# Strassen's sums from a list of their own, stores at one place, reciprocals in two pairs

## The chip, the cores and the metric

The kernel runs on one core of a Trainium2 chip. The metric is the device time of one execution in microseconds (us); of the kernel before there are three timed runs and one more under the profiler. All computation is in float32. TensorE (PE in the rows) multiplies matrices into PSUM; DVE (VectorE) and POOL (GpSimd) do elementwise work, DVE alone of the two on PSUM too; ACT (ScalarE) does activations and copies; SP (SyncE) issues nearly all transfers, in one queue. Every engine works its instructions strictly in the order of the program and waits where an operand isn't ready.

## The reference

```python
scores = scale * np.matmul(q, k.transpose(0, 1, 3, 2))        # 8 batches, 8 heads, 576 x 576
thresh = np.max(scores, axis=-1, keepdims=True) - tau
scores = np.where(scores >= thresh, scores, -1000000000.0)
attn = softmax(scores); x = attn @ v                          # bridged to (8, 576, 512)
xn = (x - mu) / np.sqrt(var + 1e-06) * g_ln
out = x + np.maximum(xn @ w_ch1, 0.0) @ w_ch2                 # 512 -> 2048 -> 512
```

## The kernel before

**Slots.** The attention of a batch runs in nine slots, s0 to s8, so there are 72 slots (`n`). A slot takes 128 queries for each of four blocks: s0 to s3 and s5 to s8 a pair of heads each, first half and second half of the sequence, s4 the leftover rows. Per slot: TensorE computes the scores into `sc`; DVE takes the maxima (`neg`, L399); ACT the exponentials `e` (L410); DVE masks them by the threshold and sums them into `den` (`weights`, L417, four instructions) and takes the reciprocal (L421); POOL divides `e` by `den` (L430, four instructions); DVE turns the 32x32 blocks into `et` (L495, two instructions, L489 in s4); SP writes `et` to a scratch in DRAM (`scr`, four transfers) and in the next slot reads it back as `em` (L510). TensorE multiplies `em` with V (L539) late in that next slot. In the first batch the weights are turned on TensorE instead, with diagonal matrices `diag`.

**Groups.** The sequence of a batch is two groups of 288 tokens, so there are 16 groups. A group's feed-forward part is cut into small steps, which `second_part` issues between the attention's matmuls, four times per slot (quarters 0 to 3). A group's mean is subtracted on DVE (`xc`, L580), then `p` = xc times W1 (4096 matmuls in all), relu on ACT into `hidden`, and the second product in Strassen's form: seven quarter products (`seg`) instead of eight, with sums and differences t1 to t4 of the quarters of `hidden` made on the way (L746), and the seven results, copied from PSUM by ACT, summed into `y` on POOL (L766), multiplied by the inverse deviation `rb` on DVE (L772) and added to x on POOL. `y` is turned on DVE (`ot`, L603) and stored by 16 transfers (L610). The first group has a plain second product.

The second group of a batch is ready two slots into the next batch: it has its `p` products from s2 to s4 there and its quarter products in s4 to s6. The first group of a batch starts in s6 and has its quarter products from the end of s8 to s1 of the next batch. The former is called an odd group below, the latter an even one (by its number).

**Order.** Everything that isn't TensorE's waits in lists of calls: `aside` (sums, differences, `root`, `store`) is run whole at four places of a slot, `stores` (the 16 transfers) at two, at the start of a slot and behind `weights`. Whatever a place runs is put into the engines' queues there, ahead of what the program issues later. So the list decides which work of the feed-forward part stands ahead of the attention's on DVE, POOL and SP.

Of the kernel before, what the change touches and what calls it, by code (L numbers as in the profile page):

```python
# [12 lines left out]
ALU = mybir.AluOpType  # L13
# [5 lines left out]
def kernel(  # L19
# [392 lines left out]
    def weights(es, thr, divide):  # L412
# [8 lines left out]
        nc.vector.reciprocal(den, den)  # L421
        diags = []
        for i in range(4):
            if not divide:
                if i % 2 == 0:
                    two = ffn.tile([128, TOK], F32, tag="o", bufs=6, name="diag")
# [160 lines left out]
    aside, stores = [], []  # L587
# [7 lines left out]
    def add_to_x(g, m, p2, rb):  # L595
        o = ffn.tile([128, TOK], F32, tag="o", bufs=6, name="o")
# [4 lines left out]
    def store(g, m, o):  # L601
        ot = ffn.tile([128, TOK], F32, tag="o", bufs=6, name="ot")
# [114 lines left out]
    def second_quarters(g, rb):  # L717
# [12 lines left out]
        def later(*calls):  # L730
            for what, fn, *args in calls:
# [5 lines left out]
                aside.append(go)  # L737

        def need(*what):
            while not done.issuperset(what):  # L740
                run_all(aside)
# [6 lines left out]
        def segment(weights, rhs, out=None):  # L748
# [10 lines left out]
            if out is None:  # L759
                out = ffn.tile([128, TOK], F32, tag="o", bufs=6, name="o")  # L760
                out = out.rearrange("p (m t) -> p m t", m=HM)
# [3 lines left out]
        def add(out, a, b):  # L765
            side.tensor_tensor(out=out, in0=a, in1=b, op=ALU.add)  # L766

        def finish(i, j):

            z = part_of(y, i, j)  # L770
            r = rb[:, (early, late)[j]].unsqueeze(1).to_broadcast([128, HM, HT])
            nc.vector.tensor_tensor(out=z, in0=z, in1=r, op=ALU.mult)  # L772
            add(z, z, part_of(groups[g], i, j))

        def give(i):
            for m in range(HM * i, HM * i + HM):
                store(g, m, y[:, m])

        side = nc.gpsimd
        later(("t3", by_fours, nc.gpsimd, b12, b22, b12, ALU.subtract))  # L780
        yield from segment(w2[0, 0], b11, y11)
        later(("t2", by_fours, nc.vector, b11, b11, b12, ALU.add))
        yield 2, 0.5
        p2 = yield from segment(w2[0, 1], b21)
        later(("t4", by_fours, nc.gpsimd, b21, b21, b11, ALU.subtract))
        yield 2, 0.5
        need("t3")
        p7 = yield from segment(s3, b12)
        yield 2, 0.5
        need("t2")  # L790
        yield from segment(s2, b11, y21)
        need("t4")
        later(
            ("t1", by_fours, nc.vector, b11, b22, b11, ALU.subtract),
            ("u2", add, y21, y21, y11),
            ("11", add, y11, y11, p2),
# [3 lines left out]
        later(("done11", finish, 0, 0))  # L800
# [4 lines left out]
            ("u4", add, y12, y21, p5), ("u3", add, y21, y21, p7), ("22", add, y22, y21, p5),  # L805
# [194 lines left out]
```

## Time and profile before

| | |
|---|---|
| timed runs, median (lowest to highest) | 1494.86 us (1493.07 to 1495.52) |
| profiled execution | 1493.05 us, span 1491.3 us |
| granted TensorE clock, mean | 0.982 |
| busy: PE, DVE, POOL, ACT | 91%, 63%, 43%, 31% of the span |
| TensorE's idle time before L539 (product with V) | 53.2 us |
| before the `p` products (L101) | 19.8 us, 14.3 of it waiting for `xc` |
| before the quarter products (L101) | 9.9 us |
| transfers: HBM read, written | 119.41 MB, 83.76 MB |

A row of a timeline has start, duration (us), engine, line, operation, output<-input, shapes, number of instructions, and in brackets the idle time ahead of it with what ended it. A row of the groups has total busy time, mean ns of one, and the idle time ahead with what ended most of it. In rows of a table by windows the third column from the end is TensorE's granted clock.

### The profile page before, as it was taken

How to read it: one execution, taken by the hardware profiler on the slowest of the kernel's cores; microseconds unless marked ns; L12 is line 12 of the kernel's file. 1: busy time of each engine (PE TensorE's matmuls, PEld its weight loads, DVE VectorE, ACT ScalarE, POOL GpSimd, SP SyncE). 2: the span in 40 equal slices, each digit the busy share in tenths (PEclk: the TensorE clock that was granted, in tenths of full speed). 3: DMA queues.
4: the chain of work that ended last, by engine and by line, in shares of the span. 5: the costliest groups of instructions: out<-in, count | busy, mean ns of one | idle time of the engine just before them, and what ended most of it. 6: DMA issues, size and time to landing. Idle time of an engine off the chain costs nothing.

```text
span 1491.3 us, 36015 instructions
## 1 busy us (share of the span) xinstructions
PE 1361.4 (91%) x15048; PEld 1008.2 (68%) x15048; DVE 934.4 (63%) x1560; ACT 459.4 (31%) x923; POOL 635.7 (43%) x854
## 2 busy tenths in 40 slices
PE   5879998999999898989999889998989889999996
PEld 3656665768576585857768576675858667685866
DVE  5989867567665674657755666556755576555421
ACT  3886422232322222222322323222232222323120
POOL 2354435545444352444535345343534444353413
PEclk8999999999999999999999999999999999999998
DMA  9612475468653887449744577447874487545211
GB/s 220 175 57 80 98 167 138 129 161 176 153 150 98 175 178 175 117 105 190 172 134 129 139 168 169 131 113 176 182 169 125 110 173 177 136 129 127 82 17 17
DMA packets 466868, 205.53 MB, mean 138 GB/s; under 512 B 275025, under 2 KB 428369, under 8 KB 466705
## 3 DMA queue, kind: packets, MB, share of 16 engines
q1 hardware_dynamic: 461936, 202.64, 56.9%
q8 instruction: 118, 1.93, 0.6%
q10 hardware_dynamic: 4736, 0.59, 0.4%
q14 instruction: 46, 0.37, 0.1%
q0 software_dynamic: 32, 0.00, 0.0%
HBM read 119.41 MB, written 83.76 MB: 136 GB/s over the span
## 4 chain that ended last, share of the span: by engine, by line
PE 48%; DVE 18%; DMA 12%; POOL 9%; SPq 6%; issue 4%; ACT 2%; DVEq 0%; POOLq 0%; ACTq 0%
PE seg L101 17%; PE p L101 15%; PE sc L539 8%; PE sc L385 7%; DVE e L417 6%; DMA scr<-et 5%; DMA em<-scr 5%; POOL y L766 4%; POOL e L430 4%; DVE et L495 3%; SPq L501 2%; DVE neg L399 2%; SPq L116 2%; DVE xc L580 1%; PE tp L101 1%
## 5 line engine op out<-in xcount | busy, mean ns | idle before, releaser
L101 PE MATMUL p<-xc,w 128*64 128x288 f32 x4096 | 524.3, 410 | 19.8 <-DVE xc L580 14.3
L101 PEld LDWEIGHTS p<-xc,w 128*64 128x64 f32 x4096 | 300.4, 138 | 226.8 <-issue 29.5
L399 DVE TENSOR_REDUCE neg<-sc 128x2 f32<-128x1152 f32 x144 | 188.4, 1349 | 241.0 <-PE sc L385 241.0
L430 POOL TENSOR_SCALAR e<-e,den 128x576 f32<-128x576 f32 x252 | 196.5, 796 | 213.4 <-DVE den L421 213.4
L410 ACT ACTIVATE e<-sc,neg 128x576 f32<-128x576 f32 x288 | 196.4, 742 | 264.7 <-DVE neg L399 257.9
L101 PE MATMUL seg<-hidden,w 128*64 128x144 f32 x3840 | 249.2, 287 | 0.0
L101 PEld LDWEIGHTS seg<-hidden,w 128*64 128x64 f32 x3840 | 235.7, 137 | 12.4 <-issue 7.7
L417 DVE SCALAR_TENSOR_TENSOR e<-sc,thr,e 128x576 f32<-128x576 f32 x288 | 219.1, 810 | 10.4 <-ACT e L410 10.4
L495 DVE STREAM_TRANSPOSE et<-e 128x1152 f32<-128x1152 f32 x112 | 151.9, 1369 | 83.2 <-POOL e L430 68.1
L539 PE MATMUL sc<-em,v_in 128*64 128x256 f32 (+1 forms) x1408 | 142.4, 348 | 53.2 <-DMA em<-scr 35.2
L682 ACT ACTIVATE hidden<-p 128x288 f32<-128x288 f32 x256 | 105.7, 413 | 225.2 <-PE p L101 223.4
L385 PE MATMUL sc<-kT,qT 64*128 64x384 f32 (+3 forms) x1024 | 150.6, 425 | 20.1 <-DVE qT L345 10.1
L403 POOL TENSOR_SCALAR thr<-neg,low_sb 128x2 f32<-128x2 f32 x144 | 43.1, 299 | 287.6 <-DVE neg L399 285.4
L539 PEld LDWEIGHTS sc<-em,v_in 128*64 128x64 f32 x1408 | 93.5, 142 | 91.6 <-DVE sq L628 26.8
L385 PEld LDWEIGHTS sc<-kT,qT 64*128 64x128 f32 x1024 | 94.2, 191 | 69.9 <-issue 16.1
L101 PE MATMUL seg<-hidden,stage 128*64 128x144 f32 x1920 | 123.4, 287 | 2.7 <-POOL hidden L746 2.7
L101 PEld LDWEIGHTS seg<-hidden,stage 128*64 128x64 f32 x1920 | 118.0, 137 | 6.5 <-POOL hidden L746 3.0
L556 ACT COPY x<-sc 128x256 f32<-128x256 f32 x60 | 22.3, 371 | 247.2 <-PE sc L539 241.1
L746 POOL TENSOR_TENSOR hidden<-hidden 128x576 f32<-128x576 f32 x60 | 85.1, 1437 | 23.0 <-ACT hidden L682 15.1
L772 DVE TENSOR_TENSOR y<-y,rb 128x288 f32<-128x288 f32 x60 | 35.5, 592 | 94.8 <-POOL y L766 94.8
L565 POOL TENSOR_TENSOR sum<-sum,x 128x256 f32<-128x256 f32 (+1 forms) x64 | 35.7, 557 | 121.3 <-ACT x L556 118.8
L766 POOL TENSOR_TENSOR y<-y,o 128x288 f32<-128x288 f32 x90 | 79.3, 881 | 14.0 <-ACT o L762 9.3
(149 smaller groups left out, 1177.9 us busy)
## 6 DMA issues: line engine op xcount, KB each, us to landing
scr<-et SPq DMA_DIRECT2D x252, 288.0 KB, 4.6
em<-scr SPq DMA_DIRECT2D x63, 1024.0 KB, 5.9
out_dram<-ot SPq DMA_DIRECT2D x256, 36.0 KB, 2.1
q_in<-in_q_dram SPq DMA_DIRECT2D x124, 72.0 KB, 5.5
k_in<-in_k_dram SPq DMA_DIRECT2D x120, 72.0 KB, 3.1
v_in<-in_v_dram SPq DMA_DIRECT2D x64, 128.0 KB, 4.5
rest<-scr SPq DMA_DIRECT2D x63, 128.0 KB, 6.0
w<-in_moe_w_ch_dram SPq DMA_DIRECT2D x10, 512.0 KB, 6.1
```

Source lines behind the costliest of these rows:

```text
L101: nc.tensor.matmul(out[r], lhsT=lhsT[:, r], rhs=rhs, **flags)
L385: nc.tensor.matmul(sc[h][64 * i : 64 * i + 64 if s == HP else 128, at : at + n], lhsT=ql[r] if s == HP else qT[r, half, j * 128 : (j + 1) ...
L399: nc.vector.tensor_reduce(out=neg[:, i], in_=pairs[h], axis=AXL.X, op=ALU.max, negate=True,)
L403: nc.gpsimd.tensor_scalar(out=thr[:, i], in0=neg[:, i], scalar1=-1.0, scalar2=low_sb, op0=ALU.mult, op1=ALU.add,)
L410: nc.scalar.activation(es[:, i], blocks[i], func=AF.Exp, bias=neg[:, i : i + 1])
L417: nc.vector.scalar_tensor_tensor(out=es[:, i], in0=blocks[i], scalar=thr[:, i : i + 1], in1=es[:, i], op0=ALU.is_ge, op1=ALU.mult, accum_o ...
L430: nc.gpsimd.tensor_scalar(out=es[:, i], in0=es[:, i], scalar1=den[:, i : i + 1], scalar2=1.0, op0=ALU.mult, op1=ALU.mult,)
L495: nc.vector.transpose(et[:, :, 64 * h : 64 * h + 64].rearrange("p n (j c) -> p j n c", j=2), es[:, 2 * h : 2 * h + 2].rearrange("p j (n c) ...
L539: nc.tensor.matmul(dst[64 * h : 64 * h + 64], lhsT=vt[:, c, h, :] if c < J else vr[:, h, :], rhs=pick(em[:, c] if c < J else er, hp, h), s ...
L682: nc.scalar.activation(hidden[:, d], p1, func=AF.Relu)
L746: eng.tensor_tensor(out=out[at], in0=in0[at], in1=in1[at], op=op)
L766: side.tensor_tensor(out=out, in0=a, in1=b, op=ALU.add)
```

## The change

Three things are changed.

1. `weights`: from the second batch on, the reciprocal is taken in two instructions, one for each pair of blocks, each right behind its pair's masks.
2. The sums, differences and stores of Strassen's form leave `aside` for a list of their own, `drops`. `drip(most)` first runs everything up to and with the last urgent call (t1 to t4 are urgent), then at most `most` further ones. It is called behind `weights` with 0, behind the turning into `et` with 5, and at the end of a slot with 6. `need` takes calls from the front, one at a time. From slot 13 on, `aside` isn't run behind the maxima any more. From the second batch on, stores are issued at the start of a slot alone.
3. Who sums: the two sums that come early stay on POOL, with their multiplication and addition of x. The last five sums, and the multiplication and addition of the block that comes last, go to DVE. The second half of `y` (features 256 to 511) is multiplied and added to x by POOL in two large operations, 128x576. The results of the quarter products get a ring of four buffers of their own (`part`), and the ring `o` (`o`, `ot`, `diag`) shrinks from six to four.

```diff
+            if divide and i % 2:
+                nc.vector.reciprocal(den[:, i - 1 : i + 1], den[:, i - 1 : i + 1])
+        if not divide:
+            nc.vector.reciprocal(den, den)
...
+    def drip(most):
+        for d in [d for d in drops if d[0]]:
+            at = drops.index(d)
+            for _, fn in drops[: at + 1]:
+                fn()
+            del drops[: at + 1]
+        for _, fn in drops[:most]:
+            fn()
+        del drops[:most]
...
         def need(*what):
             while not done.issuperset(what):
-                run_all(aside)
+                drops.pop(0)[1]()
...
-        later(("t3", by_fours, nc.gpsimd, b12, b22, b12, ALU.subtract))
+        later(("t3", by_fours, pool, b12, b22, b12, ALU.subtract), urgent=True)
...
         later(
-            ("u4", add, y12, y21, p5), ("u3", add, y21, y21, p7), ("22", add, y22, y21, p5),
-            ("21", add, y21, y21, p4), ("done22", finish, 1, 1), ("done21", finish, 1, 0),
-            ("hi", aside.append, lambda: give(1)),
+            ("u4", add, dve, y12, y21, p5), ("u3", add, dve, y21, y21, p7),
+            ("22", add, dve, y22, y21, p5), ("21", add, dve, y21, y21, p4),
+            ("hi", finish, pool, 1),
         )
         yield 2, 0.5
         p3 = yield from segment(s4, b22)
-        later(
-            ("12", add, y12, y12, p3), ("done12", finish, 0, 1),
-            ("lo", aside.append, lambda: give(0)),
-        )
+        later(("12", add, dve, y12, y12, p3), ("done12", finish, dve, 0, 1))
+        later(*((f"o{m}", store, g, m, y[:, m]) for m in range(NK)))
...
-        run_all(aside)
+        if n < SLOTS + HP:
+            run_all(aside)
...
         run_all(aside)
-        run_all(stores)
+        drip(0)
+        if n < SLOTS:
+            run_all(stores)
...
         run_all(aside)
+        drip(5)
...
         run_all(aside)
+        drip(6)
```

The order of TensorE's instructions is the same in both kernels. At three places the order of the others moves.

DVE in s6 of an odd group, before (`sc_146` and `sc_147` are the two halves of the scores, `e_101` the weights):

```order
L399 TENSOR_REDUCE neg<-sc_147 128x2
L580 TENSOR_TENSOR xc<-x,mean 128x288 x4
L417 SCALAR_TENSOR_TENSOR e_101,den<-sc_146,thr,e_101 128x576 x2
L417 SCALAR_TENSOR_TENSOR e_101,den<-sc_147,thr,e_101 128x576 x2
L421 RECIPROCAL den<-den 128x4
L772 TENSOR_TENSOR y<-y,rb 128x2x144 x3
L495 STREAM_TRANSPOSE et<-e_101 128x2x18x32 x2
L603 STREAM_TRANSPOSE ot<-y 128x288 x4
L399 TENSOR_REDUCE neg<-sc_146 128x2
```

and in the changed kernel:

```order
L399 TENSOR_REDUCE neg<-sc_147 128x2
L583 TENSOR_TENSOR xc<-x,mean 128x288 x4
L417 SCALAR_TENSOR_TENSOR e_101,den<-sc_146,thr,e_101 128x576 x2
L422 RECIPROCAL den<-den 128x2
L417 SCALAR_TENSOR_TENSOR e_101,den<-sc_147,thr,e_101 128x576 x2
L422 RECIPROCAL den<-den 128x2
L498 STREAM_TRANSPOSE et<-e_101 128x2x18x32 x2
L779 TENSOR_TENSOR y<-y,part 128x2x144 x5
L787 TENSOR_TENSOR y<-y,rb 128x2x144
L779 TENSOR_TENSOR y<-y,x 128x2x144
L617 STREAM_TRANSPOSE ot<-y 128x288 x4
L399 TENSOR_REDUCE neg<-sc_146 128x2
```

The turning into `et` now follows the reciprocals directly, and the work on `y` stands behind it.

SP from the middle of s2 to s4, before:

```order
L610 DMA out_dram<-ot 32x9x32 x8
L116 DMA q_in<-in_q_dram 32x18x32 x4
L116 DMA k_in<-in_k_dram 32x18x32 x4
L610 DMA out_dram<-ot 32x9x32 x8
L501 DMA scr<-et 32x18x128 x4
L510 DMA em<-scr 128x4x512
L511 DMA rest_94<-scr 64x512
L501 DMA scr<-et 32x18x128 x4
```

and in the changed kernel:

```order
L624 DMA out_dram<-ot 32x9x32 x12
L116 DMA q_in<-in_q_dram 32x18x32 x4
L116 DMA k_in<-in_k_dram 32x18x32 x4
L504 DMA scr<-et 32x18x128 x4
L513 DMA em<-scr 128x4x512
L514 DMA rest_94<-scr 64x512
L624 DMA out_dram<-ot 32x9x32 x4
L504 DMA scr<-et 32x18x128 x4
```

Four stores more stand ahead of the loads of q and k, none between these and `scr`, and four behind the next `em`.

POOL in s5 of an odd group, before (`hidden<-hidden` is t4, one instruction for each half):

```order
L403 TENSOR_SCALAR thr<-neg,low_sb 128x2 x2
L746 TENSOR_TENSOR hidden<-hidden 128x4x144 x2
L430 TENSOR_SCALAR e_101<-e_101,den 128x576 x4
L766 TENSOR_TENSOR y<-y 128x2x144
L766 TENSOR_TENSOR y<-y,o 128x2x144
```

and in the changed kernel:

```order
L403 TENSOR_SCALAR thr<-neg,low_sb 128x2 x2
L433 TENSOR_SCALAR e_101<-e_101,den 128x576 x4
L760 TENSOR_TENSOR hidden<-hidden 128x4x144 x2
L779 TENSOR_TENSOR y<-y 128x2x144
L779 TENSOR_TENSOR y<-y,part 128x2x144
L787 TENSOR_TENSOR y<-y,rb 128x2x144
```

t4 and the division have changed places.

More of the change, by code (lines that the diff above doesn't have):

```diff
@@ L775, in give, with add, finish @@
[L775 to L779, printed above, removed]
[L780 removed]
+        def add(eng, out, a, b):
+            eng.tensor_tensor(out=out, in0=a, in1=b, op=ALU.add)
+        def finish(eng, i, j=None):
+            cols = slice(None) if j is None else (early, late)[j]
+            at = (slice(None), slice(HM * i, HM * i + HM), cols)
+            z, x = y[at], groups[g][at]
+            r = rb[:, cols].unsqueeze(1).to_broadcast(list(z.shape))
+            eng.tensor_tensor(out=z, in0=z, in1=r, op=ALU.mult)
+            add(eng, z, z, x)
```

42 lines of the change are left out of this document (17 added, 25 removed).

## The prediction

> **What bounds the kernel now.** I read the busy shares first, then TensorE's groups with what ended their idle time, then TensorE's timeline over one batch, and behind each gap the queues of DVE, POOL and SP. TensorE is busy for 91% of the span, so the time is its work plus its gaps. Two groups of gaps count:
>
> ```profile
> L101 PE MATMUL p<-xc,w 128*64 128x288 f32 x4096 | 524.3, 410 | 19.8 <-DVE xc L580 14.3 <-ACT hidden L682 3.8 <-DVE o L597 0.7
> L539 PE MATMUL sc<-em,v_in 128*64 128x256 f32 (+1 forms) x1408 | 142.4, 348 | 53.2 <-DMA em<-scr 35.2 <-DVE rb L629 6.8 <-DVE et L495 5.9
> ```
>
> 53.2 us before the product with V (L539), which needs the turned weights `em`, and 14.3 us before the first product of a group, which needs the centred x (`xc`). In TensorE's timeline of one batch (about 174 us, which the next batches repeat) they are:
>
> ```profile
> 664.53 1.95 PE L539 MATMUL sc<-em,v_in 128*64 128x256 f32 x16 [2.81 <-DMA em<-scr]
> 685.26 1.95 PE L539 MATMUL sc<-em,v_in 128*64 128x256 f32 x16 [2.71 <-DVE rb L629]
> 728.95 12.01 PE L101 MATMUL p<-xc,w 128*64 128x288 f32 x96 [1.64 <-DVE xc L580]
> 761.49 2.77 PE L539 MATMUL sc<-em,v_in 128*64 128x256 f32 x16 [2.75 <-DVE sq L628]
> 808.88 4.14 PE L101 MATMUL seg<-hidden,e 128*64 128x144 f32 x64 [1.20 <-ACT o L762]
> ```
>
> The first four stand in slots s7, s8, s2 and s3. Two name DVE, but TensorE also waits for a transfer there: `em` is issued at 678.97 and 755.87 (below), and a transfer of it takes
>
> ```profile
> DMA to landing us min/median/max: 5.5/6.1/6.6
> ```
>
> so it lands at about 685.1 and 761.4 or later, when TensorE starts. The fifth gap is a PSUM bank's copy and stays.
>
> Why `em` is late in s7 (made from the weights of s6), on DVE, then POOL, then SP's queue:
>
> ```profile
> 638.11 0.18 DVE L421 RECIPROCAL den<-den 128x4 f32<-128x4 f32 x1
> 643.83 0.46 DVE L772 TENSOR_TENSOR y<-y,rb 128x288 f32<-128x288 f32 x1 [5.55 <-POOL y L766]
> 644.98 1.04 DVE L772 TENSOR_TENSOR y<-y,rb 128x288 f32<-128x288 f32 x1 [0.69 <-POOL y L766]
> ...
> 648.07 2.63 DVE L495 STREAM_TRANSPOSE et<-e 128x1152 f32<-128x1152 f32 x2
> 650.63 1.51 DVE L603 STREAM_TRANSPOSE ot<-y 128x288 f32<-128x288 f32 x4
> 652.07 2.58 DVE L399 TENSOR_REDUCE neg<-sc 128x2 f32<-128x1152 f32 x2
> ...
> 661.88 2.82 DVE L495 STREAM_TRANSPOSE et<-e 128x1152 f32<-128x1152 f32 x2 [3.58 <-POOL e L430]
> ```
>
> ```profile
> 638.39 2.90 POOL L430 TENSOR_SCALAR e<-e,den 128x576 f32<-128x576 f32 x4 [4.86 <-DVE den L421]
> 641.26 3.69 POOL L766 TENSOR_TENSOR y<-y,o 128x288 f32<-128x288 f32 x4
> 644.91 0.79 POOL L766 TENSOR_TENSOR y<-y,x 128x288 f32<-128x288 f32 x1
> ```
>
> ```profile
> 658.54 0.38 SPq L510 DMA_DIRECT2D em<-scr  x1
> ...
> 659.52 10.88 SPq L610 DMA_DIRECT2D out_dram<-ot  x16
> 670.51 3.89 SPq L501 DMA_DIRECT2D scr<-et  x4
> ...
> 678.97 0.45 SPq L510 DMA_DIRECT2D em<-scr  x1
> ```
>
> POOL has divided all weights at 641.29, but the three multiplications of `y` stand ahead of the turning (`et`) on DVE and wait for POOL's sums, so `et` begins at 648.07 instead of 641.3. The lateness is handed on: sixteen stores (10.88 us) wait for that `em`, and the next `scr` stands behind them until 670.51, although its `et` was ready at 664.70. That is the gap in s8.
>
> **The change part by part.**
>
> *Reciprocals in pairs.* One more reciprocal (0.18 us) per slot on DVE, about 0.2 us later for the last two weights. POOL starts on the first pair two weights earlier; after the last reciprocal two divisions remain instead of four. By POOL's row (2.90 us for four) `et` ends 1.45 us minus the extra 0.2, 1.25 us, earlier where nothing else stands ahead. In s7 the squares' sums stand ahead of the division on POOL (`et` waits 3.58), and nothing is gained.
>
> *Sums behind `et`, in s6.* Weights end at 638.1; the second pair is divided by about 639.9, `et` runs until 641.3 instead of 650.7: 9.4 us. Behind it DVE now has seven operations, five sums, a multiplication and the addition of x (0.46 us each alone, 3.2), and four `ot` (1.5 us before), of which two wait for POOL's two large operations. Those are 128x576, bounded below by the 128x288 row (0.8) and above by POOL's 128x576 sum,
>
> ```profile
> L746 POOL TENSOR_TENSOR hidden<-hidden 128x576 f32<-128x576 f32 x60 | 85.1, 1437 | 23.0 <-ACT hidden L682 15.1 <-PE seg L101 7.1 <-DVE hidden L746 0.8
> ```
>
> so 1.6 to 2.9 us; I take 2.9, the same shape. DVE ends near 647.5. The maxima of s7 (L399) are queued behind; in the trace they began at 652.07, so 4.5 us cover this, and gone they would delay s7's weights. A DVE operation beside one of POOL's took 1.04 instead of 0.46 (644.98, beside POOL's 644.91). With all seven so, 4.1 us more, DVE would end at 651.6, no later than in the trace. [...]
>
> So `em` of s6 is there about 9 us early and the 2.81 us go. The stores follow that `em`, from about 650.4, and end at 661.3, before the next `et` (664.70). That `scr` goes at 664.7 instead of 670.51, 5.8 us earlier, and its `em` lands at 679.45 instead of 685.26. TensorE, 2.81 us earlier, wants it at 685.26 - 2.71 - 2.81 = 679.74. The margin of 0.3 us is thinner than the spread of landings, so I leave 0.5 us in each of six batches, 3.0.
>
> *s1 to s3.* In s1 the `xc` operations stood behind a multiplication that waited for POOL's sums. Now they stand behind four DVE sums: the turning of s1, whose `scr` is issued at 723.30 (next rows), ends 1.25 us earlier, near 722.0; four sums (0.46 to 1.04 each) and `xc` (24.6 us for 64 by L580, 0.4 each) end between 725.5 and 727.8. TensorE is free for them at 728.95 - 1.64 = 727.31. I take the 1.64 as gone; by the upper end 0.5 us would stay. Then SP's queue:
>
> ```profile
> 723.30 3.76 SPq L501 DMA_DIRECT2D scr<-et  x4
> ...
> 731.52 0.46 SPq L510 DMA_DIRECT2D em<-scr  x1
> ...
> 732.59 6.28 SPq L610 DMA_DIRECT2D out_dram<-ot  x8
> ...
> 743.92 3.93 SPq L610 DMA_DIRECT2D out_dram<-ot  x8
> 747.95 3.89 SPq L501 DMA_DIRECT2D scr<-et  x4
> 755.87 0.38 SPq L510 DMA_DIRECT2D em<-scr  x1
> ```
>
> ```profile
> 739.90 2.82 DVE L495 STREAM_TRANSPOSE et<-e 128x1152 f32<-128x1152 f32 x2 [1.60 <-POOL e L430]
> ```
>
> The `scr` at 747.95 is held by the queue, not by its `et` (done at 742.72). It comes 1.25 us earlier because the chain ahead does (pairs), and 3.93/2 = 1.95 earlier because four stores move behind it: 3.2 in all. The four go behind the next `em`, where that product waits for nothing. TensorE, relieved of 1.64, asks 1.64 earlier, so of the two gaps together 3.2 is gained and the rest stays. The waits in s3 over the batches:
>
> ```profile
> 412.80 1.95 PE L539 MATMUL sc<-em,v_in 128*64 128x256 f32 x16 [3.31 <-DMA em<-scr]
> 587.58 2.93 PE L539 MATMUL sc<-em,v_in 128*64 128x256 f32 x16 [4.07 <-DVE rb L629]
> 939.08 2.86 PE L539 MATMUL sc<-em,v_in 128*64 128x256 f32 x16 [2.62 <-DVE sq L628]
> 1113.66 3.35 PE L539 MATMUL sc<-em,v_in 128*64 128x256 f32 x16 [3.94 <-DMA em<-scr]
> ```
>
> With 761.49's 2.75, and 1.65 added and 3.2 taken from each: 1.8 + 2.5 + 1.1 + 2.4 + 1.2 = 9.0 us stay.
>
> *A new wait in s5.* The difference t4 (two POOL operations on `hidden`) stood ahead of the division, and stands now behind it:
>
> ```profile
> 792.44 0.18 DVE L421 RECIPROCAL den<-den 128x4 f32<-128x4 f32 x1
> ```
>
> ```profile
> 789.31 2.81 POOL L746 TENSOR_TENSOR hidden<-hidden 128x576 f32<-128x576 f32 x2
> 792.73 2.91 POOL L430 TENSOR_SCALAR e<-e,den 128x576 f32<-128x576 f32 x4 [0.61 <-DVE den L421]
> ```
>
> ```profile
> 794.56 3.85 PE L101 MATMUL seg<-hidden,w 128*64 128x144 f32 x60
> ```
>
> POOL's pairs run from 791.1 to 794.3 (the second pair is ready near 792.8), t4's first half ends at 795.8, and TensorE wants it at 794.56: 1.3 us. The second half (797.2) is wanted two us after the first. Bounds: 0 if the division starts at once and runs short, 2.6 if it begins no earlier than now and TensorE waits until 797.1. I take 1.3, in six groups (3 to 13): 7.8 us.
>
> *The clock.* Some gaps are followed by slow matmuls. The granted clock (third column from the end) over the 9 us behind two of them:
>
> ```profile
> 761.49:770.50 9.01, 9.01 (x76) 5.80 (x76) 0.19 (x1) 1.19 (x3) 0.73 (x1) 0.81 0.74 210
> 412.80:422.00 9.20, 9.20 (x92) 5.95 (x94) 1.87 (x3) 1.19 (x3) 0.96 (x2) 1.00 0.74 212
> ```
>
> 0.81 over 9 us is 1.7 us lost. Nine gaps, of 2.2 us and more, are followed by 0.80 to 0.82, and none below 2.2. Eight of them vanish or shrink below that or near it: 8 x 1.7 = 13.6 us. [...]
>
> *Buffers.* Parts get four buffers of their own, stores four: five parts and four `ot` per group, each reused tens of us later; no cost, and bounded by the one place in the first batch where `o` and the diagonals share them (a wait of a few us off TensorE's path).
>
> **Sum** against the profiled execution, 1493.05 us (span 1491.3), which lies 1.8 below the median of the runs: gaps 53.2 + 14.3 = 67.5, of which 9.0 + 3.0 stay: -55.5. Clock -13.6. t4 +7.8. Together -61.3, so 1431.7; I say **1432**.
>
> **The rivals.**
> - *The queue takes the gains back* (1460). Stores, loads and `scr` go through one queue, and if `scr` and `em` land later when they meet the stores, s8 and s3 keep their waits. Then the s7 waits (2.8 x 7 = 19.7), the 14.3 and half the clock (6.8) are gained, less 7.8: 33. For it: the margin of 0.3 us in s8. Against: 5.8 us of SP's row are waiting, not moving.
> - *t4 costs more* (1449). If it waits 2.6 us and drops the clock (1.7), 4.3 x 6 = 26 instead of 7.8.
> - *Better* (1415): t4 hidden (-7.8) and no rest in s3 (-9.0).
> - *It doesn't do what it says* (1487): the gaps that name DVE are DVE's and the others stay late by other causes, so only 14.3 - 7.8 = 6.5 is gained. Against: `em`'s issue plus 6.1 meets TensorE's start within 0.5 us.
> - *Slower: the transfers are the bound* (1503). Where `em`, `scr` and the stores meet earlier on the transfer engines (0.74 busy behind 761.49 and 412.80), each `em` lands 3 us later. s8 and s3 keep their waits and get 3 us more in six batches, 36; s7 (19.7) and `xc` (14.3) are still gained and t4 pays 7.8: 36 - 34 + 7.8 = +10. It decides from 2.2 us per `em`, where the three cancel. Against: landings spread over only 1.1 us, collisions included.
>
> **How the numbers follow.** Forecast 0.58, queue 0.15, t4 0.12, better 0.08, nothing done 0.04, slower 0.03. The range 1414 to 1466 holds the first four. About 0.2% can be told from no change, and half of "nothing done" may fall within it: faster 0.95, same 0.02, slower 0.03.
>
> **What would show it.** In the changed trace: no gap ahead of L539 in s7; `scr` right behind its `et` in s7; a gap of 1 to 2.4 us in s3; none ahead of `xc`; a new gap of about 1.3 us with POOL's `hidden` as releaser in s5; clock 1.00 behind nearly all gaps. It is wrong if the gap in s7 stays, if `scr` in s7 still waits for stores, or if maxima (L399) start later after their scores than now.

## The result and the profile after

The changed kernel takes **1436.24 us** (median; 1433.86 to 1439.93) beside 1495.19 us of the kernel before on the same chip: ratio **0.9605**, 95% interval 0.9575 to 0.9634. The profiled execution took 1436.73 us, its span is 1435.0. The forecast was 1432 in a range of 1414 to 1466.

TensorE is busy for 1345.6 us (94% of the span), before 1361.4 (91%). Its three groups of which the prediction spoke now read:

```profile
L101 PE MATMUL p<-xc,w 128*64 128x288 f32 x4096 | 519.9, 408 | 13.3 <-ACT hidden L696 11.1 <-DVE o L611 0.9 <-ACT sq L709 0.6
L101 PE MATMUL seg<-hidden,w 128*64 128x144 f32 x3840 | 249.3, 287 | 5.9 <-POOL hidden L760 5.9
L542 PE MATMUL sc<-em,v_in 128*64 128x256 f32 (+1 forms) x1408 | 134.3, 335 | 14.6 <-DMA em<-scr 10.8 <-DVE sq L642 2.3 <-DVE rb L635 1.5
```

The idle time before the product with V (L542) fell from 53.2 to 14.6 us, and the wait for `xc` left the list. In its place stands a wait for `hidden` from L696, ScalarE's relu: 11.1 us, before 3.8. The difference t4 (POOL's `hidden`) now costs 5.9. Of TensorE's gaps in its timeline of the middle batches, one of each kind:

```profile
603.27 3.90 PE L101 MATMUL seg<-hidden,w 128*64 128x144 f32 x60 [0.98 <-POOL hidden L760]
709.39 7.98 PE L101 MATMUL p<-xc,w 128*64 128x288 f32 x64 [1.21 <-ACT hidden L696]
781.85 4.14 PE L101 MATMUL seg<-hidden,e 128*64 128x144 f32 x64 [1.20 <-ACT part L775]
902.93 3.68 PE L542 MATMUL sc<-em,v_in 128*64 128x256 f32 x16 [3.91 <-DMA em<-scr]
```

No gap of s7 or s8 is left in any batch. DVE in s6 shows what is different there: `et` starts 0.2 us after the last reciprocal (before, 9.96 us after it), and the list runs behind it and is done before the next scores. Whether the place or the engine of the sums did this, these rows can't tell; the experiments can.

```profile
620.99 0.17 DVE L422 RECIPROCAL den<-den 128x2 f32<-128x2 f32 x1
621.19 1.38 DVE L498 STREAM_TRANSPOSE et<-e 128x1152 f32<-128x1152 f32 x1
622.75 1.38 DVE L498 STREAM_TRANSPOSE et<-e 128x1152 f32<-128x1152 f32 x1 [0.18 <-POOL e L433]
624.05 2.26 DVE L779 TENSOR_TENSOR y<-y,part 128x288 f32<-128x288 f32 x5
634.30 2.62 DVE L399 TENSOR_REDUCE neg<-sc 128x2 f32<-128x1152 f32 x2 [3.23 <-PE sc L385]
```

SP's queue in the same stretch: the sixteen stores are over before the next `scr`, and that one goes right behind its `et` (done at 646.98).

```profile
632.94 10.82 SPq L624 DMA_DIRECT2D out_dram<-ot  x16
647.01 3.80 SPq L504 DMA_DIRECT2D scr<-et  x4
```

**The new wait in s2.** TensorE's scores of s2 end where its next `p` products begin, at 704.08 (the first row below). The maxima behind them start 2.2 us later, because the list's second place stands ahead of them on DVE; so the exponentials start late on ScalarE, and the relu that must free a PSUM bank stands behind two of them.

```profile
704.08 4.10 PE L101 MATMUL p<-xc,w 128*64 128x288 f32 x32
```

```profile
704.57 0.46 DVE L779 TENSOR_TENSOR y<-y,x 128x288 f32<-128x288 f32 x1
705.13 1.20 DVE L617 STREAM_TRANSPOSE ot<-y 128x288 f32<-128x288 f32 x3
706.25 2.58 DVE L399 TENSOR_REDUCE neg<-sc 128x2 f32<-128x1152 f32 x2
```

And ScalarE:

```profile
707.66 1.37 ACT L410 ACTIVATE e<-sc,neg 128x576 f32<-128x576 f32 x2 [5.15 <-DVE neg L399]
708.93 0.71 ACT L696 ACTIVATE hidden<-p 128x288 f32<-128x288 f32 x2
```

TensorE goes on at 709.39 (above). This happens in six batches, 7.3 us together.

The lateness of these maxima is not new. In the trace before they start even 2.5 us after their scores, in each of the six batches:

```profile
725.09 2.21 PE L385 MATMUL sc<-kT,qT 64*128 64x384 f32 x16
729.81 2.61 DVE L399 TENSOR_REDUCE neg<-sc 128x2 f32<-128x1152 f32 x2
```

But there TensorE stood 1.64 us for `xc` behind the scores and began the products at 728.95, only 0.86 us ahead of the maxima. The wait for `xc` hid this one; with it gone, the relu is wanted earlier than ScalarE gets to it.

The books of the two profiled executions, spans 1491.3 and 1435.0, difference 56.3:

| TensorE | before, us | after, us | difference |
|---|---|---|---|
| idle before the product with V | 53.2 | 14.6 | -38.6 |
| idle before `p`: `xc` | 14.3 | 0.3 | -14.0 |
| idle before `p`: relu (`hidden`) | 3.8 | 11.1 | +7.3 |
| idle before `seg`: POOL's `hidden` | 2.7 | 6.0 | +3.3 |
| busy (the same matmuls; mean granted clock 0.982 before, 0.989 after) | 1361.4 | 1345.6 | -15.8 |
| sum | | | -57.8 |

The rest, +1.5 us, is idle time of other groups of TensorE: all its idle time fell by 40.5 us (129.9 to 89.4), the four groups of the table by 42.0.

### The profile page after: what moved, and what is told of

The parts are those of the page before. It is cut to its first block, busy times and chain, and to the rows that moved or that the text cites. A ratio compares the mean times of both kernels' runs of the same rounds, so it can differ in the third digit from the quotient of the medians.

```text
span 1435.0 us, 35948 instructions
## 1 busy us (share of the span) xinstructions
PE 1345.6 (94%) x15048; PEld 993.2 (69%) x15048; DVE 997.7 (70%) x1668; ACT 459.3 (32%) x923; POOL 599.5 (42%) x779
## 4 chain that ended last, share of the span: by engine, by line
PE 67%; DVE 11%; DMA 6%; SPq 5%; ACT 4%; POOL 2%; issue 2%; DVEq 0%; ACTq 0%; POOLq 0%
PE p L101 28%; PE seg L101 20%; PE sc L542 9%; PE sc L385 8%; DVE e L417 3%; DMA scr<-et 3%; DVE neg L399 3%; ACT e L410 3%; SPq L116 3%; DMA em<-scr 2%; SPq L504 1%; POOL e L433 1%; PE tp L101 1%; DMA rest<-scr 1%; POOL hidden L760 1%
## 5 line engine op out<-in xcount | busy, mean ns | idle before, releaser
L101 PE MATMUL p<-xc,w 128*64 128x288 f32 x4096 | 519.9, 408 | 13.3 <-ACT hidden L696 11.1
L101 PEld LDWEIGHTS p<-xc,w 128*64 128x64 f32 x4096 | 293.7, 137 | 221.1 <-ACT hidden L696 24.1
L101 PE MATMUL seg<-hidden,w 128*64 128x144 f32 x3840 | 249.3, 287 | 5.9 <-POOL hidden L760 5.9
L696 ACT ACTIVATE hidden<-p 128x288 f32<-128x288 f32 x256 | 104.9, 413 | 220.6 <-PE p L101 219.1
L385 PE MATMUL sc<-kT,qT 64*128 64x384 f32 (+3 forms) x1024 | 150.6, 425 | 20.0 <-DVE qT L345 10.1
L542 PE MATMUL sc<-em,v_in 128*64 128x256 f32 (+1 forms) x1408 | 134.3, 335 | 14.6 <-DMA em<-scr 10.8
L542 PEld LDWEIGHTS sc<-em,v_in 128*64 128x64 f32 x1408 | 88.4, 139 | 49.7 <-DVE rb L643 6.3
L760 POOL TENSOR_TENSOR hidden<-hidden 128x576 f32<-128x576 f32 x60 | 88.4, 1492 | 23.1 <-ACT hidden L696 15.1
L568 POOL TENSOR_TENSOR sum<-sum,x 128x256 f32<-128x256 f32 (+1 forms) x64 | 32.7, 510 | 131.8 <-ACT x L559 129.3
L760 DVE TENSOR_TENSOR hidden<-hidden 128x576 f32<-128x576 f32 x60 | 60.2, 1039 | 30.0 <-PE seg L101 27.4
L775 ACT COPY part<-seg 128x288 f32<-128x288 f32 x75 | 30.0, 400 | 142.8 <-PE seg L101 138.5
```

Source lines behind the costliest of these rows:

```text
L101: nc.tensor.matmul(out[r], lhsT=lhsT[:, r], rhs=rhs, **flags)
L385: nc.tensor.matmul(sc[h][64 * i : 64 * i + 64 if s == HP else 128, at : at + n], lhsT=ql[r] if s == HP else qT[r, half, j * 128 : (j + 1) ...
L542: nc.tensor.matmul(dst[64 * h : 64 * h + 64], lhsT=vt[:, c, h, :] if c < J else vr[:, h, :], rhs=pick(em[:, c] if c < J else er, hp, h), s ...
L696: nc.scalar.activation(hidden[:, d], p1, func=AF.Relu)
L760: eng.tensor_tensor(out=out[at], in0=in0[at], in1=in1[at], op=op)
```

## The experiments

The theory that the prediction used is called "place" in the expectations: what stands ahead of `et` on DVE, or ahead of `scr` in SP's queue, makes `em` late, and the change moves it behind. The rivals are named there. All times in one table; each ratio is to the kernel before, run between on the same chip, and the last columns come from each run's profile. Not all rows were run on the same chip, so between two rows the ratios are the safer comparison. By them the run with the list ahead lies 17 us below the changed kernel (16 by the medians), the one with one reciprocal 22 above it (24), and the one with t4 first 7 below it (10).

| kernel | median us | ratio (95%) | idle before V | idle before `p` | PE busy |
|---|---|---|---|---|---|
| the changed one | 1436.24 | 0.9605 (0.9575 to 0.9634) | 14.6 | 13.3 | 1345.6 |
| before + pairs | 1476.81 | 0.9868 (0.9830 to 0.9906) | 45.6 | 12.1 | 1354.9 |
| before + stores at one place | 1471.36 | 0.9847 (0.9819 to 0.9876) | 30.9 | 19.7 | 1363.0 |
| before + both of these | 1448.58 | 0.9690 (0.9662 to 0.9719) | 28.5 | 12.1 | 1352.8 |
| before + late sums on DVE | 1464.19 | 0.9798 (0.9773 to 0.9822) | 35.5 | 18.4 | 1357.1 |
| changed, sums on POOL | 1454.34 | 0.9723 (0.9707 to 0.9738) | 5.6 | 29.3 | 1354.2 |
| changed, list ahead of `et` | 1420.24 | 0.9492 (0.9475 to 0.9508) | 9.6 | 6.0 | 1341.3 |
| changed, one reciprocal | 1460.57 | 0.9752 (0.9720 to 0.9784) | 14.6 | 17.7 | 1359.1 |
| changed, t4 first | 1426.33 | 0.9557 (0.9529 to 0.9585) | 11.7 | 13.3 | 1346.1 |
| changed, list's second place behind the next maxima | 1483.52 | 0.9924 (0.9895 to 0.9952) | 49.3 | 5.9 | 1357.4 |
| the same, t4 first | 1475.83 | 0.9885 (0.9857 to 0.9913) | 49.6 | 6.0 | 1354.7 |
| the same as the last but one, stores at once | 1441.12 | 0.9635 (0.9603 to 0.9667) | 25.9 | 6.0 | 1348.3 |
| changed, list ahead of `et`, t4 first | 1413.55 | 0.9455 (0.9428 to 0.9482) | 7.8 | 6.0 | 1340.0 |

### One edit alone: the pairs

```diff
-        nc.vector.reciprocal(den, den)
+            if divide and i % 2:
+                nc.vector.reciprocal(den[:, i - 1 : i + 1], den[:, i - 1 : i + 1])
+        if not divide:
+            nc.vector.reciprocal(den, den)
```

> The kernel before, with only the reciprocals in two pairs. Theory 'place' (operations of DVE that stand ahead of et and wait make em late; stores in the queue hand the lateness on): the pairs give each em about 1.25 us, in s7 too, because POOL's sums start that much earlier; three PV waits and the xc wait of a batch shrink by 1.25 us each at most, and no gap vanishes. 6 x 1.25 to 6 x 3.75 us, so 1470 to 1488, middle 1480. Theory 'pairs' (the earlier start of the division carries most of the 59 us): 1445 to 1455, and the gaps of s7 and s8 are under 1 us.

1476.81 us, 20 less than before, inside the range of "place". The gaps of s7 stay but shrink, by 0.5 to 2.0 us in six batches; the five of s8 are 12.6 us together as before, and those of s3 in the same batches grow from 16.7 to 19.4 us, likely because TensorE gets there earlier. The `xc` wait that stood at 1.64 is

```profile
717.40 12.01 PE L101 MATMUL p<-xc,w 128*64 128x288 f32 x96 [0.41 <-DVE xc L583]
```

1.23 us shorter, the 1.25 that the prediction worked out for the pairs. The pairs are not the main thing, but alone they are worth a third of the change.

### One edit alone: the stores

```diff
         run_all(aside)
-        run_all(stores)
+        if n < SLOTS:
+            run_all(stores)
         tick(3)
```

> The kernel before, with only the second sending place (behind the weights) taken away from the second batch on, so that stores leave only behind an em issue. Theory 'place': s7's em is as late as before, the four stores of s2 leave the way of that slot's scr (3.93/2 = 1.95 us earlier), so s3's gap shrinks by up to 1.95 in five batches, less where the gap falls under 2.2 us and the clock stays: 1480 to 1490, middle 1485. Theory 'queue' (the stores ahead of scr are what makes em late everywhere): 1455 to 1470.

1471.36 us, 23.5 less: twice the middle of "place" and below its range, though "queue" is not met either. From the third batch on, the gaps of s3 (2.62 to 4.07 us before) went whole, where the expectation had 1.95 us for four stores. In this kernel all eight stores of the second place leave the way of that `scr`, not four. It is issued 6.64 us earlier in the trace than before (747.95), while the `p` products ahead begin 2.79 us earlier (726.16 and 728.95): 3.85 us are gained, the 3.93 that the eight stores had taken.

```profile
741.31 3.98 SPq L501 DMA_DIRECT2D scr<-et  x4
```

The gaps of s8 went too, in four of the five batches that had one; only in the second batch did these two slots lose by it (s3 went from 2.24 to 3.87 us, s8 from 0 to 3.84). SP's queue and TensorE show how in one of them:

```profile
656.04 0.38 SPq L510 DMA_DIRECT2D em<-scr  x1
...
657.02 9.79 SPq L610 DMA_DIRECT2D out_dram<-ot  x16
666.91 3.97 SPq L501 DMA_DIRECT2D scr<-et  x4
...
675.42 0.45 SPq L510 DMA_DIRECT2D em<-scr  x1
```

```profile
662.14 2.74 PE L539 MATMUL sc<-em,v_in 128*64 128x256 f32 x16 [2.89 <-DMA em<-scr]
```

The sixteen stores took 9.79 us to issue instead of 10.88, and s8's `em` goes out 13.28 us after s7's product started instead of 14.44 (678.97 - 664.53). And behind s7's gap the matmuls now run slowly (2.74 us for sixteen instead of 1.95; the granted clock over the 9 us behind the gap is 0.81, before 1.00), so TensorE asks for that `em` 19.53 us after s7's start (at 681.67) instead of 18.02. 1.16 + 1.51 = 2.67, nearly the 2.71 of the old gap. So in this batch part of a vanished gap is TensorE's own lateness and no gain; such lateness shows in the busy time, 1363.0 us, the highest of all these kernels. The other batches weren't worked out like this.

### The two together

> The kernel before with both small edits, the reciprocals in pairs and one sending place for the stores; the sums stay on POOL, ahead of et. If the gains of the two (about 18 and 24 us alone) add, 1453 (1448 to 1458): then they carry 42 of the change's 59 us, and the list no more than 17. Theory 'place' as it was forecast (the sums behind et carry s7 and s8) expects them to overlap little and the gap of s7 to stay at 2 to 3 us. Theory 'one chain': both relieve the same em, so the second adds less than half of its 24: 1462 to 1472.

1448.58 us, 47.4 less (the diff is the two above). The gains add, 20.3 + 23.5 = 43.8. "One chain", by which the second edit would add less than half, falls. Of the change's 59 us these two small edits carry 47. The gaps of s7 are still there, at 1.4 to 2.1 us.

### One edit alone: the late sums on DVE

```diff
-        def add(out, a, b):
-            side.tensor_tensor(out=out, in0=a, in1=b, op=ALU.add)
+        def add(out, a, b, eng=nc.vector):
+            eng.tensor_tensor(out=out, in0=a, in1=b, op=ALU.add)
```

with `nc.gpsimd` given for the first sums, u2, 11 and done11, as before.

> The kernel before with only the engine of the late sums changed: ten operations of POOL (five sums, three additions of x a group, of two kinds) on DVE at their old places ahead of et; one reciprocal, two sending places. Theory 'engine' (et waited because DVE's multiplications waited for POOL's sums, not because work stood ahead of it): eleven operations of 0.46 us, 5.1, run from 638.3 while POOL divides (2.9), et begins at 643.4 instead of 648.1, more than the 2.81 of s7's gap; s7's gap goes in six batches, s8's in part, s3's stay: 1460 to 1478, middle 1470. Theory 'place' (what stands ahead of et is what counts): with 0.46 to 1.04 each et begins at 643 to 650, gaps as before: 1488 to 1500.

1464.19 us, 32 less. This is "engine", and it contradicts "place": all eleven operations still stand ahead of `et` on DVE,

```profile
634.15 0.18 DVE L421 RECIPROCAL den<-den 128x4 f32<-128x4 f32 x1
634.24 3.18 DVE L766 TENSOR_TENSOR y<-y,o 128x288 f32<-128x288 f32 x4
...
640.38 0.46 DVE L766 TENSOR_TENSOR y<-y,x 128x288 f32<-128x288 f32 x1
640.76 2.63 DVE L495 STREAM_TRANSPOSE et<-e 128x1152 f32<-128x1152 f32 x2
```

but `et` begins 6.6 us after the reciprocal instead of 9.96, and s7's product waits 0.16 us instead of 2.81:

```profile
657.71 1.95 PE L539 MATMUL sc<-em,v_in 128*64 128x256 f32 x16 [0.16 <-DMA em<-scr]
```

The gaps of s8 and s3 stay (3.17 and 2.44 in that batch). The `xc` wait halves (14.3 to 7.0), and the relu wait of s2 appears here too (3.8 to 9.2). What held `et` in s6 was not the work ahead of it but the stall in that work, for POOL's sums, which themselves stood behind the division.

### Place and engine apart

In the changed kernel, the late sums back on POOL, at the list's places:

```diff
-            ("u4", add, dve, y12, y21, p5), ("u3", add, dve, y21, y21, p7),
-            ("22", add, dve, y22, y21, p5), ("21", add, dve, y21, y21, p4),
+            ("u4", add, pool, y12, y21, p5), ("u3", add, pool, y21, y21, p7),
+            ("22", add, pool, y22, y21, p5), ("21", add, pool, y21, y21, p4),
...
-        later(("12", add, dve, y12, y12, p3), ("done12", finish, dve, 0, 1))
+        later(("12", add, pool, y12, y12, p3), ("done12", finish, pool, 0, 1))
```

> The changed kernel with all its sums on POOL, at the places of the changed list (behind et). Theory 'place': et and em are untouched, no gap before V in s7; what waits for POOL now is ot, and the maxima of s7 and s2 behind it: seven operations of 0.8 to 0.9 us on POOL, 6 us, of which about 4.5 are covered; 1438 to 1455, middle 1443. Theory 'engine': em and xc wait for POOL as before, 1465 to 1490.

1454.34 us, at the upper end of "place". Before V only 5.6 us are left, the least of all: behind `et` the sums can't harm `em`, whoever makes them. The price is paid in s2. The `ot` wait for POOL, the maxima stand behind them, and they start 4.9 us after their scores (end at 709.0):

```profile
712.78 1.20 DVE L617 STREAM_TRANSPOSE ot<-y 128x288 f32<-128x288 f32 x3 [7.69 <-POOL y L779]
713.90 2.58 DVE L399 TENSOR_REDUCE neg<-sc 128x2 f32<-128x1152 f32 x2
```

```profile
717.04 9.55 PE L101 MATMUL p<-xc,w 128*64 128x288 f32 x64 [3.95 <-ACT hidden L696]
```

In the changed kernel, the list's first place ahead of `et`:

```diff
-        drip(0)
+        drip(5)
         if n < SLOTS:
...
         run_all(aside)
-        drip(5)
```

> The changed kernel with the list's first place, five operations, ahead of the turning (et) instead of behind it; engines of the sums and pairs as changed. Theory 'place': five sums on DVE, 0.46 to 1.04 us each, stand ahead of et in s6 and s1, less the 1.4 us in which POOL still divides: et 1 to 4 us later. With margins of 0.6 (s7) and 1.6 us (s8) the gaps of s7 come back with 0.5 to 3.4 us in each batch, and gaps above 2.2 us take the clock with them: 1445 to 1465, middle 1453. Theory 'engine' (what made em late was that DVE waited for POOL's sums; sums on DVE itself cost nothing anywhere): 1434 to 1440.

1420.24 us: faster than the changed kernel by 16 us, on the far side of both theories. "Place" is refuted here; "engine" has the direction but not the size. DVE in s6:

```profile
616.07 0.17 DVE L422 RECIPROCAL den<-den 128x2 f32<-128x2 f32 x1
616.15 2.77 DVE L779 TENSOR_TENSOR y<-y,part 128x288 f32<-128x288 f32 x4
618.84 2.63 DVE L498 STREAM_TRANSPOSE et<-e 128x1152 f32<-128x1152 f32 x2
```

Four sums ahead of `et` move its start from 0.2 to 2.8 us behind the reciprocal, and its end from 3.1 to 5.4 us behind it. The product with V in s7 doesn't see these 2.3 us. The expectation had given its `em` only 0.6 us to spare, and that was the mistake. In the changed kernel that `em` is issued 12.4 us ahead of the product, and `em` takes 5.4 to 7.4 us to land in that trace, so some 5 us are to spare:

```profile
631.95 0.38 SPq L513 DMA_DIRECT2D em<-scr  x1
644.36 1.90 PE L542 MATMUL sc<-em,v_in 128*64 128x256 f32 x16
```

What the sums no longer do is stand ahead of the next maxima. In s2 those start 0.1 us after their scores,

```profile
698.92 2.62 DVE L399 TENSOR_REDUCE neg<-sc 128x2 f32<-128x1152 f32 x2 [0.35 <-PE sc L385]
```

and the relu wait is gone (idle before `p` 6.0 us, of it ACT's `hidden` 3.8, as before the change). Counted from the start of the `p` products, the maxima of s2 are 0.1 us late here, 0.86 in the kernel before, 1.84 in the run with late sums on DVE, 2.2 in the changed kernel, 3.1 with one reciprocal and 4.9 with sums on POOL. The relu waits there are 0, 0, 0.92, 1.21, 2.14 and 3.95 us: each time the lateness less about 0.95, or nothing. That chain is shown.

The 16.7 us between the two spans are 7.3 ahead of `p`, 5.0 ahead of V and 4.3 of busy time. Ahead of V, s3 loses 8.0 us and small gaps in other slots take 3.1. That the gaps of s3 shrank because their `em` starts from these maxima is likely, but no run tests it alone.

With pairs and one sending place in all four, the table of place and engine is therefore: sums on POOL ahead of `et` 1448.6, on POOL behind it 1454.3, on DVE behind it 1436.2, on DVE ahead of it 1420.2. (The first differs from the others in more things: t4 stands ahead of the division, the last multiplications are DVE's, and there are no large operations for the second half of `y`.) Behind `et` the engine is worth 18 us, and with the sums on DVE the place behind `et` costs 16. The other two differences, 28 and 6, carry what else the first kernel has, and the 6 is not clear of the noise (the intervals overlap).

### The pairs taken out of the change

The first diff of this section, undone in the changed kernel.

> The changed kernel with one reciprocal for all four columns again; order on every engine otherwise as changed. Theory 'place': em is 1.25 us later where its margin is thin. In the changed kernel s7's em lands about 0.6 us before it is wanted, s8's about 1.6, s3's late, t4 0.98 late: 0.65 + 0 + 1.25 + 1.25 per batch, 6 x 3.15 = 19 us, so about 1455 (1445 to 1465). Theory 'pairs': 1475 or more, the PV waits back at 40 us.

1460.57 us, 24 more, as "place" had it within 6. But not where it had them: the idle time before V is 14.6 us in all, what it was, though the single gaps differ. The groups name other places:

```profile
L101 PE MATMUL p<-xc,w 128*64 128x288 f32 x4096 | 525.1, 411 | 17.7 <-ACT hidden L693 15.6 <-DVE o L608 0.7 <-ACT sq L706 0.6
L101 PE MATMUL seg<-hidden,w 128*64 128x144 f32 x3840 | 257.7, 293 | 14.0 <-POOL hidden L757 14.0
```

t4, behind the division, comes 1.35 us later: 2.34 us in each of six batches instead of 0.98, 14.0 in all. Behind five of these six gaps the granted clock over 9 us is 0.81 or 0.82 (behind the sixth 1.00), and `seg` is busy 257.7 us instead of 249.3. The relu wait grew by 4.5. Waits 8.1 + 4.5 and busy time 13.5 make 26.1 us, as much as the two spans differ (1461.1 and 1435.0).

### t4 ahead of the division again

```diff
         if n < SLOTS + HP:
             run_all(aside)
+        drip(0)
         tick(1)
```

> The changed kernel with the difference t4 ahead of POOL's division of the weights again, as before; nothing else moves on any engine. Theory 'place': the six waits of 0.98 us for t4 go, 5.9 us; the division of that slot is up to 2.8 us later, and that slot's em has the margin: 1430 to 1432. Rival: that em is then late and the product with V one slot later waits 1 to 2 us in six batches: 1436 to 1448.

1426.33 us, 10 less than the changed kernel, 7 by the ratios, whose intervals overlap a little. It is below the range of "place" (1430 to 1432), and the rival, a late `em`, is out. The six waits are gone, 5.9 us, and idle before V is 11.7, 2.9 less; the gaps of s3 vary, and nothing shows that t4's move caused this part. The two spans differ by 8.1 us (1435.0 and 1426.9), about what these two come to.

### The list's second place behind the next maxima

```diff
         next(rest, None)
+        if not any(d[0] for d in drops):
+            drip(6)
...
         run_all(aside)
-        drip(6)
+        drip(0)
```

> The changed kernel with the list's second place, six operations, moved from the end of a slot to behind the next slot's maxima (neg). Theory 'place' (the relu of s2 stands behind exponentials that wait for neg, and neg stands behind six list operations on DVE): neg of s2 starts right behind its scores, 2.2 us earlier; the six waits of 1.22 us for hidden by L696 go, 7.3 us, and the twelve stores fall behind the next scr, so that the 14.6 us before V in s3 shrink to 5 or less: 1418 to 1430, middle 1424. Rival: the six operations (3.7 us) now stand ahead of s2's weights, which start 1 to 2 us later, and s3 waits more than it gains: 1436 to 1450.

1483.52 us: nearly all of the gain is lost, worse than both theories. The relu waits went as forecast (idle before `p` 5.9), but

```profile
L542 PE MATMUL sc<-em,v_in 128*64 128x256 f32 (+1 forms) x1408 | 142.9, 349 | 49.3 <-DMA em<-scr 47.6 <-DVE et L492 1.6
```

The `ot` are made some 9 us later against the maxima, miss the one sending place of s7 and go at that of s8, and there they stand ahead of the loads of q and k for the next batch:

```profile
666.22 10.78 SPq L624 DMA_DIRECT2D out_dram<-ot  x16
677.11 2.01 SPq L116 DMA_DIRECT2D q_in<-in_q_dram  x4
679.16 2.12 SPq L116 DMA_DIRECT2D k_in<-in_k_dram  x4
681.38 3.99 SPq L504 DMA_DIRECT2D scr<-et  x4
```

DVE waits for that k, s8's weights stand behind it, and a slot later TensorE waits:

```profile
683.26 0.78 DVE L336 STREAM_TRANSPOSE kT<-k_in 128x576 f32<-128x576 f32 x1 [3.12 <-DMA k_in<-in_k_dram]
```

```profile
695.66 3.68 PE L542 MATMUL sc<-em,v_in 128*64 128x256 f32 x16 [5.53 <-DMA em<-scr]
```

With t4 first as well it is the same picture, 1475.83 us:

> Both moves: t4 ahead of the division, the list's second place behind the next maxima. Theory 'place': the gains add, 5.9 + 7.3 + up to 10 us: 1412 to 1425, middle 1418. Rival: they share a slot's slack and the better of the two alone is not beaten.

That the stores' place is the cause, and not the six operations ahead of the weights on DVE, was then tested by sending at once:

```diff
         if not any(d[0] for d in drops):
             drip(6)
+            if n >= SLOTS:
+                run_all(stores)
```

> As the run with the list's second place behind the next maxima, which took 1483 us, but the stores are issued right behind the operations that fill them, instead of at the next slot's em: so in s7 ahead of that slot's scr, in the stretch in which SP's queue stood idle for 15 us, and not in s8 ahead of the loads of q and k. Every other engine's order is the same. Theory 'queue' (sixteen stores, 10.8 us of issue, held the loads of k and with them s8's weights, et and em): the gaps before V fall from 49.3 us to 20 or less, 1430 to 1450. Theory 'DVE' (the six operations ahead of the weights make em late): they stay above 40, 1475 to 1490.

1441.12 us: 42 us back, by moving nothing but stores within SP's queue.

```profile
643.39 7.80 SPq L624 DMA_DIRECT2D out_dram<-ot  x16
652.66 3.88 SPq L504 DMA_DIRECT2D scr<-et  x4
```

"Queue" is right in the total. The idle time before V, 25.9 us, is above the 20 that it asked: 2.1 to 3.5 us remain in s3 of five batches, and smaller gaps, up to 1.8 us, in s7 and s8.

### The better kernel

The list ahead of `et` and t4 first, both diffs above.

> The changed kernel with two moves: the list's first place ahead of et (as in the run with the list ahead, 1420 us) and t4 ahead of the division (as in the run with t4 first, 10 us less than the changed kernel). The six t4 waits of 0.99 us go and nothing else moves: 1412 to 1416, middle 1414. If the later division of s5 costs em its margin, as much comes back ahead of V: 1418 to 1424.

1413.55 us (1409.81 to 1417.8), 5.5% below the kernel before and 1.6% below the changed one. Nothing came back ahead of V (7.8 us). TensorE is busy for 1340.0 of 1408.7 us.

## Why the prediction was right, and where it was not

**The number was right** (1432 forecast, 1436 measured, on the profiled executions -61.3 against -56.3 us). Term by term:

- *PV waits, 53.2, of which 12.0 were to stay*: 14.6 stayed. s7 gone, as forecast. s8 was to keep 3.0 and kept nothing. s3 was to keep 1.8 + 2.5 + 1.1 + 2.4 + 1.2 = 9.0; its gaps are 2.78, 1.48, 0, 3.91 and 2.26 us, 10.4 in all: the sum held, the single values did not, and that is luck. The other 4.1 us lie in the second batch, where the forecast left nothing.
- *`xc`, 14.3 to nothing*: 0.3 stays. Right as far as it goes, but half of it was not to be had.
- *The missing term, +7.3*: the relu wait in s2. The step that failed is "I take the 1.64 as gone": I worked out what stands ahead of the maxima in s6 and s7, and never looked at them in s2. There they start 2.5 us after their scores already in the kernel before, behind the `xc` wait. Without it TensorE meets them, 1.2 us in each of six batches. The list of signs would not have caught it: it asked whether the maxima start later after their scores than before, and they start a little sooner, 2.2 us against 2.5. With this term the sum would have been -61.3 + 7.3 = -54.0, against -56.3.
- *t4, 7.8*: 5.9. Six waits in six groups, as forecast, 0.98 instead of 1.3 us each; removed by the run with t4 first. In the books the wait for POOL's `hidden` rose by only 3.3, because one of 2.7 us in the second batch went, which the sum did not have.
- *The clock, 13.6*: 15.8 less busy time. By the count below, ten gaps of the trace before, not nine, are followed by a clock of 0.81, and two of the trace after by 0.81 and 0.69. Between 2.1 and 4 us the length of a gap does not tell whether it costs clock: in the prediction's own rows 0.81 stands behind a gap of 2.75 us and 1.00 behind one of 3.31, and of the 90 gaps from 2.1 to 4 us in all traces, 60 are followed by a clock below 0.9.
- *Pairs, 1.25 us a slot*: 1.23 in the `xc` wait of the run with pairs alone, 1.35 at t4 when they are taken out. In the changed kernel they serve t4 and the relu, not `em`: without them the wait before V is no longer.
- *POOL's two large operations, 2.9 us*: 1.55 + 1.50 = 3.05 in s6. DVE was to end 9.4 us behind the weights; it ended 10.1 behind the start of the last reciprocal, and the maxima still waited 3.23 us for scores.

So the total came within 5.0 us because errors of both signs met: +7.3 (relu), +2.6 (V), +0.3 (`xc`) and +1.5 (other idle time) against -4.5 (POOL's `hidden`) and -2.2 (busy time). That it came as close as this is in part luck.

**A reason was wrong.** "Sums behind `et`, in s6 ... 9.4 us": the 9.4 us are real, but the place behind `et` is not what freed s7's product. The sums' move to DVE does it alone, ahead of `et` (run with late sums on DVE), and with DVE's sums the place behind `et` is worse by 16 us (list ahead). I had read the row that says so, a multiplication with 5.55 us of idle time ahead of it and POOL as releaser, and gave the whole time to the order of the queue and none to the wait in it. Four sums ahead of `et` take 2.8 us and make it end 2.3 us later, which the product with V has to spare; behind `et` they take time ahead of the next maxima, which have none to spare in s2.

**The stores** were put at 1.95 us per s3, for four of them. Alone they are worth 23.5 us, because in that run eight leave the way in s3 (3.85 us), and most of the s8 gaps went as well. Of the rivals, "the queue takes the gains back" was the one with substance: it did not happen in this change, since the stores fell into a stretch in which SP's queue is idle (they end at 643.76, and the next `scr` goes at 647.01), but one later slot made it real (1483 us). That the transfers themselves were the bound (the slower rival) the trace after speaks against: `em` lands 6.0 us after its issue in the median, beside 5.9 before. The spread that the prediction set against that rival, 1.1 us, is that of a part of the trace; over the whole of it landings took 5.4 to 7.8 us.

What stays open: why s3's gap is 3.91 us in one batch and 0 in another at the same order of instructions.

## What to carry to other kernels

An operation ahead of a critical one in an in-order queue costs only the time by which it holds it. Here four sums of DVE ahead of `et` made it end 2.3 us later, which s7's product did not see, while a multiplication that stood 5.55 us for POOL's sums left a gap of 2.81 us there. So give it to the engine that can run it without waiting, and put it ahead of the operation whose result has time to spare. Moving it behind is not free, for it then stands ahead of the next critical one (16 us here). For each moved operation, ask in every stage of the loop what is next in that queue, not only in the stage whose wait is to go. And for each wait that is to go, ask which other one it hides. Small transfers on a shared issue queue cost their issue time to what waits behind them (sixteen took 7.8 to 11.5 us of SP's queue, and in the kernel before a `scr` whose `et` was done at 664.70 went at 670.51), so their place is chosen by the gaps in that queue; sixteen of them moved by one slot were worth 42 us here.

## What the runs showed that was not expected

**The clock behind a gap is not set by its length alone.** Over 14 traces I took every gap of TensorE of 1.1 us and more behind the first 200 us, 276 of them, and the granted clock over the 9 us behind each. Of 170 gaps under 2.1 us four are followed by a clock under 0.9, each with a second gap of over 5 us within those 9; of the 90 from 2.1 to 4 us, 60 are; of the 16 above 4 us, all. Two of the changed kernel's (the third column from the end is the clock):

```profile
902.93:912.13 9.20, 9.20 (x64) 5.51 (x68) 0.00 (x0) 1.19 (x3) 0.72 (x1) 0.69 0.74 204
405.17:414.37 9.20, 9.20 (x92) 5.95 (x94) 1.74 (x3) 1.45 (x4) 0.96 (x2) 1.00 0.75 198
```

The gaps were 3.91 and 2.78 us. So between 2.1 and 4 us the length does not tell whether a gap costs clock, and in these traces one below 2.1 us has not cost any by itself. Just above 2.1 us most already do: 15 of the 20 from 2.1 to 2.4 us are followed by a clock under 0.9. What decides stays open.

**DVE beside POOL.** A 128x288 multiplication and addition of DVE took 1.55 us each in s6, against 0.46 alone, beside POOL operations that had begun 0.3 us earlier:

```profile
626.35 1.55 DVE L787 TENSOR_TENSOR y<-y,rb 128x288 f32<-128x288 f32 x1
627.93 1.55 DVE L779 TENSOR_TENSOR y<-y,x 128x288 f32<-128x288 f32 x1
```

```profile
626.03 1.55 POOL L787 TENSOR_TENSOR y<-y,rb 128x576 f32<-128x576 f32 x1 [3.31 <-DVE y L779]
627.66 1.50 POOL L779 TENSOR_TENSOR y<-y,x 128x576 f32<-128x576 f32 x1
```

The prediction had bounded this by 1.04. Each DVE operation ends 0.32 us after POOL's (627.90 and 627.58, 629.48 and 629.16), and so does the prediction's own row (644.98 and 1.04, beside 644.91 and 0.79). So the time of these three was set by what was left of POOL's. That of `xc` was not: its four subtractions, 128x288 too, took 1.54 us together from 700.68 on, beside a POOL operation of 1.41 us from 700.84 on. Why is not shown.

**Issue time of stores varies.** Sixteen stores of the same form took 10.88, 10.82, 10.78, 9.79 and 7.80 us of SP's queue in five kernels, and within the kernel before alone 9.56 to 11.54 us. In the traces before and after it was 9.36 or more in every row of all sixteen that began about 1 us behind an `em`'s issue; the 7.80 us are from the run with stores at once, where the `em` had been issued 6.5 us earlier (636.89, 643.39). Why is not shown.
